# Spectral MLP kernel: the opening put in another order, with bias and weight sums on GpSimd

## Chip, core and metric

The kernel runs on one core of one Trainium2 chip. The metric is the device time of one execution in microseconds; a version's time is the median of its runs.

## What is computed

```python
X = np.fft.rfft(x, axis=1)                      # x: (8, 3008, 256) f32
Yr = Xr @ w_r - Xi @ w_i + b_r                  # 256 x 256 weights
Yi = Xr @ w_i + Xi @ w_r + b_i
Y = soft_threshold(Yr, 0.01) + 1j * soft_threshold(Yi, 0.01)
y = np.fft.irfft(Y, n=3008, axis=1).reshape(24064, 256)
h = y @ w_in                                    # w_in: 256 x 2048, float64
out = np.maximum(0.01 * h, h) @ w_out           # w_out: 2048 x 256, float64
```

## The kernel before

3008 is 47 x 64, so each Fourier transform is a stage over 47 points (A, `fwd`), a stage over 64 (B, in `mid`), the complex weight product and the threshold (`proj`), and the inverse stages G (in `mid`) and the last one (`inverse`, just ahead of the MLP). Between stages the data is turned through DRAM: `fwd(b)` writes `u_dram` and `mid(b)` reads it back as `u`; `mid(b)` writes `v_dram` and `v_load` reads it as `vin`.

`mid(b)` goes over 12 pairs of frequencies. For each, TensorE does stage B into a bank `psh`; ScalarE copies it to `ef` and VectorE adds the third row of `ef`; TensorE multiplies `ef` with three weight matrices (`wr`, `wn` = -(w_r + w_i), `wd` = w_i - w_r) into a bank `pso` (then copied to `kc`) and into both halves of a bank `psf`; VectorE makes `t` = `psf` + `kc`, clamps it to `c` and subtracts `c` from `t`; ScalarE writes the parts of `t`, with signs, to `zf`; TensorE does stage G on `zf` and ScalarE copies the result to `v`, which two DMAs store. There are two banks each of `psf` and `pso`, two buffers of `kc` and three of `u`. In the later batches `t` = `psf` + `kb`, where `kb` = bias + `kc` is made by GpSimd. In batch 0 the bias comes by two more matmuls per pair: a row of ones (`ones`) against a tile `bz`, which holds the bias in two parts.

The MLP uses products of float32 in three passes of high and low parts: `yh`, `yl` against `win_hi`, `win_lo` (line 92), and `gh`, `gl` against `wout_hi`, `wout_lo` (line 576). w_in and w_out come as float64 and are converted here. `load_win(c)` loads a quarter of w_in; `convert_win(c)` splits float64 words (`float64_parts`: two reads by ScalarE, five steps by VectorE), adds the parts into `cva`, makes four sums `ws` of its quadrants for a product of seven terms, and writes high and low parts. `load_wout` does the like for w_out in eight pieces, of which the n-th is needed in the n-th step of the MLP and two steps later. `split_consts` makes high and low parts of the weights and small constants, which the batches after the first use.

The opening, lines 648 to 715, runs batch 0's `fwd`, loads and converts the quarters of w_in, runs batch 0's `mid`, weaves in batch 1's `fwd` (`stage_a1`, called turn here) and then `inverse` and `forms` for the first 512 tokens. The program text gives an order, and a scheduler places instructions on the engines by its own estimates of time; `tc.issue_after` keeps what is inside it behind a named instruction. Each engine, and each DMA queue, then works in its order. A DMA that SyncE or ScalarE starts waits, in that queue, for what it reads and for its buffer.

Tiles share buffers by `tag`: of the tag `e` there is one buffer, and of most others two.

Of the kernel before, what the change touches and what calls it, by code (L numbers as in the profile page):

```python
# [30 lines left out]
def spectral_mlp_kernel(  # L31
# [125 lines left out]
    def convert_win(c):  # L157


        a, q, s = win_tmp  # L160
        float64_parts(win_raw[c], a, q)
        dve.tensor_add(a, a, q)
        a = a.rearrange("p (j q i m) -> p j q i m", j=NH, q=2, i=2)
        a11, a12, a21, a22 = (a[:, j, :, i] for i in range(2) for j in range(2))
        dve.tensor_add(s[:, 0], a21, a22)
        dve.tensor_sub(s[:, 2], a11, a21)
        dve.tensor_sub(s[:, 1], s[:, 0], a11)
        dve.tensor_sub(s[:, 3], a12, s[:, 1])
# [6 lines left out]
    def load_wout():  # L175
# [5 lines left out]
        def load(early):  # L181
# [3 lines left out]
            with tc.issue_after(reads[13 if early else -1].ins):  # L185
                sync.dma_start(raw.rearrange("p (a f) w -> p a (f w)", a=n), ov[:, k * n:(k + 1) * n, :])
# [24 lines left out]
    reads, written, turned, turning, thresholded = [], [], [], [], []  # L211
# [4 lines left out]
    def fwd(b):  # L216
# [5 lines left out]
        def load(c):  # L222
# [89 lines left out]
    def mid(b):  # L312
# [49 lines left out]
        def proj(j):  # L362
# [4 lines left out]

            for dst, c, w in ((0, 2, "wr"), (0, 1, "wn"), (D, 0, "wd")):
# [4 lines left out]
                ] + ([((ones,), (bz[:, D if c == 0 else 0:][:, :D],))] if b == 0 and c < 2 else []))  # L373
# [3 lines left out]
                if c == 2 and b:  # L377
# [16 lines left out]
            for i in range(2):  # L394
# [4 lines left out]
                else:  # L399
                    act.mul(zf[64:, i, :], t[s, 1, :], sign[s, NK1 + j:NK1 + j + 1])  # L400
# [11 lines left out]
        def stage_g(j):  # L412
# [6 lines left out]
            for c in range(2):  # L419
                act.dma_start(vd[c, 2 * j:2 * j + 2, :N2, :].rearrange("k n d -> n k d"), v[c * N2:(c + 1) * N2])  # L420
# [238 lines left out]
    brow = sb.tile([P, 2 * D], F32, name="brow", tag="kb", bufs=1)
    for p in (0, 32):  # L660
        for r, src in enumerate((b_r, b_i)):
            sync.dma_start(brow[p:p + 1, r * D:(r + 1) * D], src.unsqueeze(0))
    sign = const.tile([P, NK1 + NPAIR], F32, name="sign")
    sync.dma_start(sign, sg)
    sync.dma_start(consts["gb32"][0], gb)

    bo = sb.tile([P, 2 * D + P], F32R, name="bz", tag="t", bufs=1)
    bz, ones = bo[:, :2 * D], bo[:, 2 * D:]
    dve.memset(ones.bitcast(F32), 1.0)
# [12 lines left out]
    with tc.issue_after(turned[0].ins):  # L682
        split_consts()
# [159 lines left out]
```

## Time and profile before

| | us |
|---|---|
| median of three runs | 2604.21 (2603.88 to 2604.37) |
| the profiled execution | 2600.34 |
| its span | 2598.6 |
| TensorE busy | 2537.5 (98%) |
| VectorE busy | 1897.1 (73%) |
| ScalarE busy | 1668.5 (64%) |
| GpSimd busy | 229.6 (9%) |

The profile is one execution. Times in it are in microseconds from the start of the span. A timeline has for each instruction its start and its length, and in brackets how long its engine had been idle and what ended that. A table of stages has for each stretch how long every engine was busy. A name as u<-u_dram is a tile with what it is made from, L343 a line of the kernel before; `x24` counts records merged into a row, of which a matmul of float32 has two. Two neighbouring instructions of VectorE overlap by some 0.08 us, so the step from one start to the next is what an instruction costs there.

### The profile page before, as it was taken

The numbers are of one execution on the slowest core, as the hardware profiler recorded it, in microseconds if no ns is written. First come the engines' busy times: TensorE is split into PE (matmuls) and PEld (weight loads), VectorE is DVE, ScalarE is ACT, GpSimd is POOL, SyncE is SP. The second block draws the span as 40 slices with busy tenths as digits, with TensorE's granted clock in tenths as the row PEclk, the third lists the DMA queues.
The fourth block names the chain that finished last, engine by engine and source line by source line (L and its number), as shares of the span: only waits on it lengthen the run. The fifth ranks groups of instructions, "written<-read, shape, count | busy, mean of one in ns | idle before, by whom it ended". The sixth has DMA issues, their size and how long they took to land.

```text
span 2598.6 us, 42643 instructions
## 1 busy us (share of the span) xinstructions
PE 2537.5 (98%) x16300; PEld 2281.5 (88%) x16300; DVE 1897.1 (73%) x3403; ACT 1668.5 (64%) x3174; POOL 229.6 (9%) x180
## 2 busy tenths in 40 slices
PE   5999999999999999999999999999999999999999
PEld 4689888999889998899988999889998889999998
DVE  7687786776777778777786777877777777767675
ACT  5766665776556666567665666566666667655564
POOL 0001121100110001100021000210002000000000
PEclk8999999999999999999999999999999999999999
DMA  8621132111221113211132111321113221101000
GB/s 259 179 85 50 48 89 72 54 47 48 82 78 49 45 41 90 75 55 51 33 97 68 49 49 37 104 67 49 49 36 101 64 58 48 44 17 32 9 17 17
DMA packets 119912, 165.13 MB, mean 64 GB/s; under 512 B 13601, under 2 KB 69917, under 8 KB 119709
## 3 DMA queue, kind: packets, MB, share of 16 engines
q1 hardware_dynamic: 79120, 115.55, 14.6%
q10 hardware_dynamic: 40589, 46.87, 7.1%
q8 instruction: 128, 2.10, 0.4%
q14 instruction: 75, 0.61, 0.1%
HBM read 86.60 MB, written 75.76 MB: 62 GB/s over the span
## 4 chain that ended last, share of the span: by engine, by line
PE 89%; DVE 3%; DMA 2%; ACT 1%; issue 0%; ACTq 0%; SPq 0%; DVEq 0%
PE pso L576 38%; PE psh L92 34%; PE psf L78 11%; PE psf L480 3%; PE psf L343 3%; DMA u<-u_dram 1%; DMA u_dram<-xin 1%; DVE yl L506 0%; DVE gl L563 0%; DMA raw<-w_out_dram 0%; DVE gf L557 0%; ACT gh L561 0%; DVE yt L511 0%; ACT gf L559 0%; DVE yc L512 0%
## 5 line engine op out<-in xcount | busy, mean ns | idle before, releaser
L92 PE MATMUL psh<-yh,win_hi 128*128 128x256 f32 x2632 | 752.3, 286 | 13.8 <-DVE gf L546 10.6
L92 PE MATMUL psh<-yl,win_hi 128*128 128x256 f32 x2632 | 738.3, 280 | 0.6 <-DVE yl L506 0.5
L92 PE MATMUL psh<-yh,win_lo 128*128 128x256 f32 x2632 | 737.9, 280 | 0.0
L576 PE MATMUL pso<-gh,wout_hi 128*128 128x512 f32 x1504 | 593.9, 395 | 0.0
L576 PE MATMUL pso<-gl,wout_hi 128*128 128x512 f32 x1504 | 591.1, 393 | 0.5 <-DVE gl L563 0.5
L576 PE MATMUL pso<-gh,wout_lo 128*128 128x512 f32 x1504 | 590.4, 393 | 0.0
L563 DVE TENSOR_TENSOR gl<-gf,gh 128x1024 fp32r<-128x1024 f32 x376 | 471.8, 1255 | 92.7 <-ACT gh L561 90.6
L92 PEld LDWEIGHTS psh<-yh,win_hi 128*128 128x128 f32 x2632 | 497.0, 189 | 30.7 <-DVE gf L546 15.4
L92 PEld LDWEIGHTS psh<-yl,win_hi 128*128 128x128 f32 x2632 | 497.0, 189 | 12.5 <-DVE yl L506 1.0
L92 PEld LDWEIGHTS psh<-yh,win_lo 128*128 128x128 f32 x2632 | 496.6, 189 | 0.2
L557 DVE TENSOR_TENSOR gf<-psh,u 128x512 f32<-128x512 f32 x376 | 259.1, 689 | 256.3 <-PE psh L92 255.1
L561 ACT CAST gh<-gf 128x1024 fp32r<-128x1024 f32 x376 | 396.4, 1054 | 7.1
L559 ACT ACTIVATE gf<-gf 128x768 f32<-128x768 f32 x376 | 320.0, 851 | 49.5 <-DVE gf L557 47.7
L576 PEld LDWEIGHTS pso<-gl,wout_hi 128*128 128x128 f32 x1504 | 282.5, 188 | 62.9 <-DVE gl L563 1.0
L576 PEld LDWEIGHTS pso<-gh,wout_hi 128*128 128x128 f32 x1504 | 283.1, 188 | 46.9 <-ACT gh L561 0.4
L576 PEld LDWEIGHTS pso<-gh,wout_lo 128*128 128x128 f32 x1504 | 282.9, 188 | 44.9
L556 ACT ACTIVATE gf<-psh 128x256 f32<-128x256 f32 x376 | 145.5, 387 | 266.6 <-PE psh L92 246.9
L542 ACT COPY p<-psh 128x256 f32<-128x256 f32 x376 | 140.1, 373 | 220.2 <-PE psh L92 219.1
L379 POOL TENSOR_TENSOR kb<-bias,kc 128x512 f32<-128x512 f32 x84 | 119.0, 1417 | 1530.6 <-ACT kc L376 1409.6
L543 DVE TENSOR_TENSOR u<-psh,p 128x256 f32<-128x256 f32 x376 | 158.6, 422 | 105.8 <-ACT p L542 103.5
L545 DVE TENSOR_TENSOR gf<-psh,u 128x256 f32<-128x256 f32 x376 | 159.3, 424 | 29.7 <-PE psh L92 2.0
L546 DVE TENSOR_TENSOR gf<-psh,gf 128x256 f32<-128x256 f32 x376 | 159.1, 423 | 9.0
(134 smaller groups left out, 3253.2 us busy)
## 6 DMA issues: line engine op xcount, KB each, us to landing
u<-u_dram SPq DMA_DIRECT2D x192, 128.0 KB, 2.7
v_dram<-v ACTq DMA_DIRECT2D x192, 128.0 KB, 2.4
out_dram<-ob SPq DMA_DIRECT2D x94, 256.0 KB, 2.1
vin<-v_dram SPq DMA_DIRECT2D x96, 240.0 KB, 3.5
xin<-x_dram SPq DMA_DIRECT2D x90, 240.0 KB, 3.0
u_dram<-xin ACTq DMA_DIRECT2D x72, 240.0 KB, 2.4
u_dram<-xin SPq DMA_DIRECT2D x24, 240.0 KB, 3.9
raw<-w_out_dram SPq DMA_DIRECT2D x8, 512.0 KB, 5.0
```

What stands on the lines that cost most here:

```text
L78: last = nc.tensor.matmul(dst, a, b, start=(i == 0), stop=(i == len(terms) - 1))
L92: mlp[:] = [nc.tensor.matmul(dst, a, b, start=start and i == 0, stop=i == 2, skip_group_check=True)]
L542: act.copy(p1, b1[:, lo])
L543: dve.tensor_add(u2, b1[:, hi], p1)
L545: dve.tensor_add(g[:, 3], b2[:, hi], u2)
L546: dve.tensor_add(g[:, 3], b2[:, lo], g[:, 3])
L556: act.activation(g[:, 0], b1[:, lo], AF.Prelu, alpha=SLOPE)
L557: dve.tensor_add(g[:, 1:3], b2.rearrange("p (k n) -> p k n", k=2), u2.unsqueeze(1).broadcast_to([P, 2, HT]))
L559: act.activation(g[:, 1:4], g[:, 1:4], AF.Prelu, alpha=SLOPE)
L561: cp = act.copy(gh, g)
L563: parted[:] = [cp, dve.tensor_sub(gl, g, gh.bitcast(F32))]
L576: mlp[:] = [nc.tensor.matmul(po, a[:, f, s], r[:, i], start=(f == 0 and j == 0), stop=(f == NF - 1 and j == 2),)]
```

## The change

Lines move by a few: what is line 379 before is line 381 after, and 165 to 168 are 167 to 170.

- The quarters 1 to 3 of w_in, the weights, the small constants and all but the first five blocks of `fb` are loaded behind the writes of `u_dram`; the rest of `fb` and quarter 1 behind the first u loads.
- The `ones` row and `bz` go. Batch 0 uses `kb` on GpSimd as the others do.
- In `convert_win` the addition and the four sums go from VectorE to GpSimd.
- Quarter 0 is converted behind the last copy of turn. Quarters 1 and 2 are converted in the middle stage behind the sign products (`signed`), quarter 3 behind the middle stage with a `cva` in the buffer of `e`. `split_consts` moves into the middle stage.
- Batch 0's stores of `v` go from ScalarE's queue to SyncE's.
- One conversion of w_out moves from ahead of the MLP into it, and its first loads are tied to the latest u load.

```diff
@@ convert_win
         a, q, s = win_tmp
+        if c == 3:
+            a = sb.tile([P, NH * NIN], F32, name="cva", tag="e", bufs=1)
         float64_parts(win_raw[c], a, q)
-        dve.tensor_add(a, a, q)
+        pool.tensor_add(a, a, q)
...
-        dve.tensor_add(s[:, 0], a21, a22)
-        dve.tensor_sub(s[:, 2], a11, a21)
-        dve.tensor_sub(s[:, 1], s[:, 0], a11)
-        dve.tensor_sub(s[:, 3], a12, s[:, 1])
+        pool.tensor_add(s[:, 0], a21, a22)
+        pool.tensor_sub(s[:, 2], a11, a21)
+        pool.tensor_sub(s[:, 1], s[:, 0], a11)
+        pool.tensor_sub(s[:, 3], a12, s[:, 1])
@@ load_wout
-            with tc.issue_after(reads[13 if early else -1].ins):
+            with tc.issue_after(reads[-1].ins):
@@ proj
-                ] + ([((ones,), (bz[:, D if c == 0 else 0:][:, :D],))] if b == 0 and c < 2 else []))
+                ])
...
-                if c == 2 and b:
                     kb = sb.tile([P, 2, D], F32, name="kb", tag="kb", bufs=1)
                     pool.tensor_add(kb, bias, kc.unsqueeze(1).broadcast_to([P, 2, D]))
...
-            c = sb.tile([P, 2, D], F32, name="c", tag="kb", bufs=1)
-            if b == 0:
-                dve.tensor_add(t, ps_y.rearrange("p (r d) -> p r d", r=2), kc.unsqueeze(1).broadcast_to([P, 2, D]))
-            else:
-                dve.tensor_add(flat(t), ps_y, flat(kb))
+            c = sb.tile([P, 2, D], F32, name="c", tag="kb" if b else "yt", bufs=1)
+            dve.tensor_add(flat(t), ps_y, flat(kb))
@@ stage_g
-                act.dma_start(vd[c, 2 * j:2 * j + 2, :N2, :].rearrange("k n d -> n k d"), v[c * N2:(c + 1) * N2])
+                (act if b else sync).dma_start(
+                    vd[c, 2 * j:2 * j + 2, :N2, :].rearrange("k n d -> n k d"), v[c * N2:(c + 1) * N2])
@@ the opening
-    load_win(0, (sync, act))
-    load_plain("fb", fb, [P, NK1 + 1, N2])
-    load_weights()
-    brow = ...
+    load_win(0, (sync, sync), xload[0])
+    consts["fb"] = const.tile([P, NK1 + 1, N2], F32, name="fb")
+    sync.dma_start(consts["fb"][:, :5], fb[:, :5])
...
     f0.finish()
-    load_win(1, (sync, sync), written[7])
+    with tc.issue_after(written[-1].ins):
+        load_weights()
+        sync.dma_start(consts["gb32"][0], gb)
...
-    convert_win(0)
     with tc.issue_after(turned[0].ins):
-        split_consts()
+        act.mul(fa32[:, 2], fa32[:, 1], -1.0)
+        convert_win(0)
     m0 = Stream(mid(0), MID)
     m0.to(0.001)
-    for c in range(2, 4):
-        load_win(c, (sync, sync), reads[3])
...
+    with tc.issue_after(reads[3].ins):
+        sync.dma_start(consts["fb"][:, 5:], fb[:, 5:])
+    load_win(1, (sync, sync), reads[3])
...
-    with tc.issue_after(turned[0].ins):
-        convert_win(1)
...
-        if i in (3, 8):
-            convert_win(2 + i // 8)
+        if i in (1, 4):
+            load_win(2 + i // 4, (sync, sync), reads[-1])
+        if i in (3, 7):
+            with tc.issue_after(signed[-1].ins):
+                convert_win(1 + i // 4)
+        if i == 9:
+            with tc.issue_after(thresholded[-1].ins), tc.issue_after(signed[-1].ins):
+                split_consts()
...
     m0.finish()
+    convert_win(3)
...
     next(wout)
-    next(wout)
```

What follows is the order of instructions at three places. First SyncE's DMA queue around the last writes of `u_dram` (`xin` to `u_dram`) and the first loads of `u`; `win_raw` are halves of a quarter of w_in, `w_105` and `w_169` hold the weights and `gb`. Before:

```order
L665 DMA w_105<-gb_dram 128x128
L267 DMA u_dram<-xin 120x512 x7
L155 DMA win_raw<-w_in_dram 128x1024
L267 DMA u_dram<-xin 120x512 x3
L155 DMA win_raw<-w_in_dram 128x1024
L267 DMA u_dram<-xin 120x512
L267 DMA u_dram<-xin 120x256 x2
L329 DMA u<-u_dram 64x2x256 x6
L155 DMA win_raw<-w_in_dram 128x1024 x4
```

After:

```order
L271 DMA u_dram<-xin 120x512 x11
L271 DMA u_dram<-xin 120x256 x2
L121 DMA w_169<-w_r_dram 128x2x256
L121 DMA w_i<-w_i_dram 128x2x256
L664 DMA w_169<-gb_dram 128x128
L333 DMA u<-u_dram 64x2x256 x6
L677 DMA bias<-b_r_dram 128x256
L677 DMA bias<-b_i_dram 128x256
L679 DMA fb<-fb_dram 128x1280
L155 DMA win_raw<-w_in_dram 128x1024 x2
```

The quarter of w_in that lay among the writes now comes behind the u loads, and the weights lie between the writes and the u loads.

Then GpSimd from the start of its work to the middle stage (`kb` is bias + `kc`, `cva` and `ws` belong to `convert_win`). Before:

```order
L317 MEMSET zero 48x256 x2
L379 ISA
L379 TENSOR_TENSOR kb<-bias,kc 128x512 x11
L317 MEMSET zero 48x256
L379 TENSOR_TENSOR kb<-bias,kc 128x512
```

After:

```order
L321 MEMSET zero 48x256
L164 ISA
L164 TENSOR_TENSOR cva<-cva,cvq 128x1024
L167 TENSOR_TENSOR ws<-cva 128x256
L168 TENSOR_TENSOR ws<-cva 128x256
L169 TENSOR_TENSOR ws<-ws,cva 128x256
L170 TENSOR_TENSOR ws<-cva,ws 128x256
L381 TENSOR_TENSOR kb<-bias,kc 128x512 x4
L164 TENSOR_TENSOR cva<-cva,cvq 128x1024
L167 TENSOR_TENSOR ws<-cva 128x256
L168 TENSOR_TENSOR ws<-cva 128x256
L381 TENSOR_TENSOR kb<-bias,kc 128x512
```

Before, its first `kb` is that of batch 1; after, the first row of work is quarter 0's addition, and a `kb` of batch 0 can stand behind the additions of a quarter.

Last VectorE where batch 0's middle stage begins (`ef` is the third row of `ef`, `win_lo` a low part of w_in, `t` and `c` belong to the threshold). Before:

```order
L348 TENSOR_TENSOR ef<-ef 128x2x128
L137 TENSOR_TENSOR cvq<-cvq,win_raw 128x1024
L348 TENSOR_TENSOR ef<-ef 128x2x128
L162 TENSOR_TENSOR cva<-cva,cvq 128x1024
L165 TENSOR_TENSOR ws<-cva 128x256
L166 TENSOR_TENSOR ws<-cva 128x256
L167 TENSOR_TENSOR ws<-ws,cva 128x256
L172 TENSOR_TENSOR win_lo<-cva,win_hi 128x2x256
L172 TENSOR_TENSOR win_lo<-cva,win_hi 128x256
L168 TENSOR_TENSOR ws<-cva,ws 128x256
L348 TENSOR_TENSOR ef<-ef 128x2x128
L172 TENSOR_TENSOR win_lo<-ws,win_hi 128x4x256
```

After:

```order
L122 TENSOR_TENSOR w_169<-w_i,w_169 128x512
L123 SCALAR_TENSOR_TENSOR w_169<-w_i,w_169 128x512
L137 TENSOR_TENSOR cvq<-cvq,win_raw 128x1024
L352 TENSOR_TENSOR ef<-ef 128x2x128 x2
L174 TENSOR_TENSOR win_lo<-cva,win_hi 128x2x256
L174 TENSOR_TENSOR win_lo<-cva,win_hi 128x256
L174 TENSOR_TENSOR win_lo<-ws,win_hi 128x4x256
L389 TENSOR_TENSOR t<-psf,kb 128x512
L390 TENSOR_SCALAR c<-t 128x512
L352 TENSOR_TENSOR ef<-ef 128x2x128
L391 TENSOR_TENSOR t<-t,c 128x512
```

Quarter 1 stood here before; after, it is quarter 0, its sums are gone from VectorE, the weights are made ready in the same place (L122, L123), and the first `t` stands behind the quarter's last piece.

## Rows read from the trace of the kernel before

**Rows 1.** The page, totals of the engines: busy us, share of span, instructions:

```profile
PE 2537.5 (98%) x16300; PEld 2281.5 (88%) x16300; DVE 1897.1 (73%) x3403; ACT 1668.5 (64%) x3174; POOL 229.6 (9%) x180
```

**Rows 2.** Stages: length, then each engine's busy us, granted clock, DMA share, GB/s:

```profile
2.00:36.40 34.40, 13.91 (x28) 5.75 (x28) 22.43 (x36) 16.89 (x30) 0.00 (x0) 0.84 0.92 293
39.90:104.50 64.60, 59.84 (x288) 48.01 (x289) 49.32 (x87) 48.23 (x96) 0.30 (x1) 0.95 0.67 192
60.00:80.00 20.00, 18.91 (x97) 14.98 (x97) 18.09 (x34) 18.33 (x38) 0.00 (x0) 1.00 0.82 247
104.50:128.70 24.20, 24.07 (x84) 13.15 (x82) 13.17 (x29) 14.81 (x32) 0.00 (x0) 0.94 0.75 220
128.70:180.00 51.30, 46.38 (x273) 39.35 (x272) 49.13 (x98) 34.16 (x63) 0.00 (x0) 0.97 0.33 96
```

**Rows 3.** Timeline of TensorE: start, us, operation, [idle before, what ended it]:

```profile
39.91 5.86 PE L343 MATMUL psh<-fb,u 128*128 128x128 f32 x24 [16.76 <-DMA u<-u_dram]
...
87.41 1.03 PE L78 MATMUL psf<-w,ef 128*128 128x256 f32 x4
88.28 1.03 PE L78 MATMUL pso<-w,ef 128*128 128x256 f32 x4
88.95 0.47 PE L78 MATMUL psf<-bz 128*128 128x256 f32 x1
89.26 1.02 PE L78 MATMUL psh<-zf,w 128*128 128x512 f32 x2
...
104.53 8.41 PE L78 MATMUL psh<-xin,fa 120*120 120x512 f32 x16
```

**Rows 4.** Timelines of ScalarE and of SyncE's DMA queue before the middle stage:

```profile
17.65 1.14 ACT L131 ACTIVATE cvq<-win_raw 128x1024 f32<-128x1024 uint32 x1 [2.17 <-DMA win_raw<-w_in_dram]
...
30.30 1.41 SPq L267 DMA_DIRECT2D u_dram<-xin  x3
36.38 3.94 SPq L329 DMA_DIRECT2D u<-u_dram  x6
```

**Rows 5.** Timeline of VectorE in the middle stage:

```profile
76.71 0.69 DVE L388 TENSOR_TENSOR t<-psf,kc 128x512 f32<-128x512 f32 x1
77.31 1.22 DVE L162 TENSOR_TENSOR cva<-cva,cvq 128x1024 f32<-128x1024 f32 x1
78.44 0.43 DVE L391 TENSOR_SCALAR c<-t 128x512 f32<-128x512 f32 x1
78.77 0.42 DVE L165 TENSOR_TENSOR ws<-cva 128x256 f32<-128x256 f32 x1
...
101.10 0.69 DVE L392 TENSOR_TENSOR t<-t,c 128x512 f32<-128x512 f32 x1
```

**Rows 6.** Timelines of VectorE and GpSimd beside each other, later batches:

```profile
333.70 1.29 POOL L379 TENSOR_TENSOR kb<-bias,kc 128x512 f32<-128x512 f32 x1 [15.01 <-ACT kc L376]
333.73 2.34 DVE L563 TENSOR_TENSOR gl<-gf,gh 128x1024 fp32r<-128x1024 f32 x1
...
372.46 2.25 POOL L246 TENSOR_TENSOR xin<-xin,xin 120x512 f32<-120x512 f32 x1
373.64 1.36 DVE L254 CAST xz<-xs 120x512 fp32r<-120x512 f32 x1
...
215.47 1.44 POOL L379 TENSOR_TENSOR kb<-bias,kc 128x512 f32<-128x512 f32 x1 [19.15 <-ACT kc L376]
215.66 0.43 DVE L546 TENSOR_TENSOR gf<-psh,gf 128x256 f32<-128x256 f32 x1
```

**Rows 7.** Groups by line and shape, whole span: count | busy us, mean ns:

```profile
L563 DVE TENSOR_TENSOR gl<-gf,gh 128x1024 fp32r<-128x1024 f32 x376 | 471.8, 1255 | 92.7 <-ACT gh L561 90.6
L254 DVE CAST xz<-xs 120x512 fp32r<-120x512 f32 x36 | 17.3, 481 | 5.6 <-PE psf L78 5.1
L246 POOL TENSOR_TENSOR xin<-xin,xin 120x256 f32<-120x256 f32 x6 | 4.5, 742 | 0.5
```

**Rows 8.** Timeline of ScalarE behind the middle stage:

```profile
116.04 0.67 ACT L131 ACTIVATE cvq<-raw 128x512 f32<-128x512 uint32 x1 [3.33 <-DMA raw<-w_out_dram]
```

More of the change, by code (lines that the diff above doesn't have):

```diff
@@ L209, in spectral_mlp_kernel @@
     v_dram = {}
-    reads, written, turned, turning, thresholded = [], [], [], [], []
+    reads, written, turned, turning, thresholded, signed, xload = [], [], [], [], [], [], []
     NX = -(-NS // 2)
@@ L234, in load @@
                 if b == 0:
-                    (act if h else sync).dma_start(t, x[b, h, :, cols])
+                    ld = (act if h else sync).dma_start(t, x[b, h, :, cols])
+                    if not h:
+                        xload[:] = [ld]
                 else:
@@ L399, in proj @@
                 else:
-                    act.mul(zf[64:, i, :], t[s, 1, :], sign[s, NK1 + j:NK1 + j + 1])
+                    signed[:] = [act.mul(zf[64:, i, :], t[s, 1, :], sign[s, NK1 + j:NK1 + j + 1])]
             if b == 0:
@@ L655, in spectral_mlp_kernel @@
     f0.to(0.01)
-    load_win(0, (sync, act))
-    load_plain("fb", fb, [P, NK1 + 1, N2])
-    load_weights()
[L659 to L662, printed above, removed]
+    load_win(0, (sync, sync), xload[0])
+    consts["fb"] = const.tile([P, NK1 + 1, N2], F32, name="fb")
+    sync.dma_start(consts["fb"][:, :5], fb[:, :5])
     sign = const.tile([P, NK1 + NPAIR], F32, name="sign")
     sync.dma_start(sign, sg)
[L665 to L669, printed above, removed]
-    dve.memset(bz.bitcast(F32), 0.0)
     f0.finish()
-    load_win(1, (sync, sync), written[7])
+    with tc.issue_after(written[-1].ins):
+        load_weights()
+        sync.dma_start(consts["gb32"][0], gb)
     pair("win", [P, 7, NQ, P])
@@ L676, in spectral_mlp_kernel @@
         sb.tile([P, 4, 2, P], F32, name="ws", tag="yh"))
-    act.copy(bz[:1], brow[:1])
-    act.copy(bz[32:33], brow[32:33])
-    dve.tensor_sub(bz[32:33], brow[32:33], bz[32:33].bitcast(F32))
-    act.mul(fa32[:, 2], fa32[:, 1], -1.0)
-    convert_win(0)
     with tc.issue_after(turned[0].ins):
-        split_consts()
+        act.mul(fa32[:, 2], fa32[:, 1], -1.0)
+        convert_win(0)
     m0 = Stream(mid(0), MID)
     m0.to(0.001)
-    for c in range(2, 4):
-        load_win(c, (sync, sync), reads[3])
     bias = const.tile([P, 2, D], F32, name="bias")
     with tc.issue_after(reads[3].ins):
-        load_plain("ga", ga, [PA, 2, P])
         for r, src in enumerate((b_r, b_i)):
             sync.dma_start(bias[:, r, :], src.unsqueeze(0).broadcast_to([P, D]))
+    with tc.issue_after(reads[3].ins):
+        sync.dma_start(consts["fb"][:, 5:], fb[:, 5:])
+    load_win(1, (sync, sync), reads[3])
+    with tc.issue_after(reads[3].ins):
+        load_plain("ga", ga, [PA, 2, P])
     fp = Stream(fwd(1), FWD)
-    with tc.issue_after(turned[0].ins):
-        convert_win(1)
     wout = load_wout()
```

## Prediction, made before the changed kernel was run

> **What bounds the kernel now.** I read the engine totals first: TensorE is busy for 98% of the span [rows 1], so whatever moves the start of the steady MLP moves the end one for one, and what stands off TensorE's path costs nothing. Then the table of stages [rows 2] with TensorE's rows [rows 3]: the idle time lies in the first 180 us. TensorE starts the middle stage at 39.91, after 16.76 us idle on the u loads, and leaves it for batch 1's turn at 104.53 [rows 3]; call this second moment M. From M to 128.7 it is full (24.07 of 24.20). From 128.7 to 180 it lacks some 5 us, with VectorE busy for 49.13 of 51.30: there VectorE is the bound, since w_out is converted beside the first MLP steps. In the middle stage three engines are close to full (TensorE 18.91, VectorE 18.09, ScalarE 18.33 of 20 in 60:80) and GpSimd does nothing [rows 2]. So relief of one engine there pays only up to the next one, and the question is whether GpSimd's time is free. The place to see that is where GpSimd works beside VectorE, in the later batches [rows 6].
>
> **Turn's writes first.** The first u load needs all 14 u_dram writes landed. The DMA engines are saturated until then, share 0.92 at 293 GB/s from 2 to 36.4 [rows 2]; SyncE has issued its last write by 31.7 and can issue the u loads only at 36.38, 3.5 us ahead of TensorE's start [rows 4, 3]. The change takes from in front of the last write 640 KB of fb, 512 KB of weights, 64 KB of gb and 1024 KB of w_in: 2.29 MB, at 293 GB/s 7.8 us. ScalarE no longer reads w_in between two turn copies, as it did at 17.65 after waiting 2.17 [rows 4], so the writes do not starve. U loads at 28.6, TensorE at 32.1. Bounds: the weights (0.59 MB, 2.0 us) now lie between the writes and the u loads; I take them as hidden in the 3.5 us, most of which is latency, and keep 0 to 2.0. The 5.86 us for the first 24 passes [rows 3] I leave as they are.
>
> **Bias off TensorE.** 24 matmuls against the ones row go. A group of four passes steps 0.87 without one (87.41 to 88.28) and 0.98 with one (88.28 to 89.26) [rows 3]: 0.11 each, 2.6 us in all, and only where TensorE is the bound. The brow loads, casts and memsets lie under the wait for DMA and cost nothing either way.
>
> **What goes to GpSimd.** Per pair one kb add of 128x512, and per quarter one add of 128x1024 and four of 128x256. GpSimd takes 1.29 for 512 columns and 0.74 for 256 [rows 6, 7], so 0.55 per 256 more and 2.4 for 1024, an estimate from these. A quarter is 2.4 + 4 x 0.74 = 5.4 us, against 1.13 + 4 x 0.33 = 2.5 on VectorE [rows 5]. Is that time free? A kb runs 1.29 from 333.70; VectorE's gl beside it, both inputs in SBUF, takes 2.34 where its mean is 1.26: it stood until GpSimd was done [rows 6, 7]. The CAST at 373.64, one SBUF input, took 1.36 beside GpSimd's add of 2.25, where its mean is 0.48 [rows 6, 7]. The addition at 215.66 reads PSUM and took its usual 0.43 beside a kb [rows 6]. So GpSimd and VectorE's SBUF-only work take turns, instruction by instruction, and only t (psf + kb) may lie beside GpSimd. I cost the two as one resource.
>
> No row has a tensor_scalar (c, L133, L134, L136) beside GpSimd; the nearest is the CAST, also with one input, and it waited, so I count them. If they did not wait, 12 x 0.33 + 8 x 0.60 = 8.8 us would leave the sum below. The Trainium skill ("SBUF — State Buffer", section Who interferes with whom) lists copy, cast and tensor_scalar as operations that can take the port pair shared with GpSimd, namely in a mode that uses both ports, and has the loser blocked for the whole instruction. By that the 8.8 us stay in the sum; no row here shows it for a tensor_scalar.
>
> **The middle stage.** VectorE, in order, stands at L122 for the weights, which land at 28.6 + 2.0 = 30.6, with quarter 0's L137 behind it: L122 and L123 1.2, L137 1.1, so 32.9. GpSimd's add 2.4 and four sums 3.0, with two ef adds and two win_lo pieces taking turns, 1.6: 39.9. ScalarE's cast of ws 1.0 and VectorE's win_lo of it 1.1 stand ahead of the first t, which so starts near 42. TensorE waits for a t only from pair 2 on. From there the shared resource has, by the steps of rows 5 (an instruction of the same length takes the same step): on VectorE 10 ef and 12 c at 0.33, 7.3; 12 subtractions at 0.60, 7.2; quarters 1 and 2, each 3 x 0.60 + 3 x 1.13 + 0.60 + 0.33 = 6.1, 12.2; the weights' splits, moved in here, 2.4; quarter 3's first three, 2.3; in all 31.4. On GpSimd 11 kb, 14.2, and quarters 1 and 2, 10.8; 25.0. Sum 56.4: without any gap it ends at 98.4. From the last subtraction (101.10 to 101.7) to M went 2.8 [rows 5, 3], so M = 101.2. But kb waits for kc, t for kb, ScalarE's casts for GpSimd, and GpSimd's add for L137 with the next kb queued behind it. VectorE was 90% busy in 60:80 [rows 2], with shorter chains than these; I take that: 56.4 / 0.90 = 62.7, M = 107.5, 3.0 **later** than before though the stage began 7.8 earlier. Bounds: 101.2 with no gap, 111.2 at 85%.
>
> SyncE takes over the 24 v writes. A u load then queues behind a v write that waits for its copy, but u loads run two pairs ahead: 0, and 1 if that cover is gone. ScalarE gets queue time back and is not the bound.
>
> **After M.** Quarter 3 still needs L136 and L137 (1.7), 5.4 on GpSimd and its casts. The third piece of w_out is loaded into the buffer of quarter 3's cva, so its load starts some 2 us later against M; ScalarE read it at 116.04 after 3.33 of waiting, ahead of the inverse's copies in order [rows 8]. Batch 1's turn covers TensorE for about 1 of the 2: +1.0, bounds 0 and 4. And one w_out piece (seven VectorE steps, 3.6) moves from the stretch behind M, where VectorE is 54% busy (13.17 of 24.20), into the one where it is 96% busy [rows 2]: between 0 and 3.6, I take +1.9 as no row tells how much of it a later step absorbs.
>
> **Sum.** 3.0 + 1.0 + 1.9 = 5.9 us on the profiled execution's 2600.3 (its span is 2598.6): 2606.2. The three timed runs have their median 3.9 above it: **2610.1**. A difference within 0.2%, 2599.0 to 2609.4, is about what a measurement of this kernel can't tell from no change.
>
> **Rivals.**
> *Faster: the turns cost little.* GpSimd's adds fall into moments when VectorE waits anyway, and the next bound decides. For TensorE that is 32.1 + 64.6 - 2.6 = 94.1. For ScalarE: 48.2 busy before [rows 2], 2.6 of splits new, from about 34, some 6 idle until the first zf and the tail of 2.8: 93.6. M 10.4 earlier, 2.9 lost after it: 2604.2 - 7.5 = 2596.7. For it: GpSimd stood idle, and kb needs only bias and kc. Against it: rows 6, and VectorE's 49.32 busy in that stage before [rows 2]. It decides once the shared work behind the first t is under some 48 us.
> *No change: turns without gaps.* M = 101.2, 3.3 earlier, 2.9 lost after: 2603.8. For it: where nothing else binds an engine can be nearly full, as VectorE in 128.7:180 [rows 2]. Against it: the chains named.
>
> **How the numbers follow.** Forecast 0.52, 0.10 of it below 2609.4; no change 0.25; faster 0.23. So faster 0.23, same 0.25 + 0.10 = 0.35, slower 0.42. Upper end: M at 111.2 gives 6.7, with 1.0 and 1.9 behind it 2613.8, and the weights' 2.0 put it at 2616. Lower end: half of the faster rival may be left out, so 2596.5.
>
> **What would show it.** The first stage-B matmul near 32: right for the writes; above 35: the DMA queue was not the cause. In the middle stage VectorE's SBUF-only operations stretched beyond their usual times, kb above 1.3 in the mean, TensorE under 85% busy, M at 106 to 109. With M below 98 the turns are cheap and the forecast is wrong. After M, the first w_in product about 1 us later against M, and the last w_out piece one MLP step later.

## The result, and the profile after

The changed kernel takes 2607.09 us in the median of 20 runs (2603.75 to 2611.10), the kernel before 2602.37 in 20 runs beside it (2599.43 to 2607.58). The ratio is 1.0019, interval 1.0012 to 1.0025: 4.7 us slower, about the 0.2% that the prediction named as the limit of what can be told. The profiled executions stand at 2606.07 and 2600.34, 5.7 us apart; the prediction had 5.9 on that scale.

The engine totals of the changed kernel, in the form of [rows 1]:

```profile
PE 2537.9 (97%) x16276; PEld 2278.0 (87%) x16276; DVE 1901.2 (73%) x3380; ACT 1663.8 (64%) x3172; POOL 276.5 (11%) x212
```

GpSimd has 46.9 us more, ScalarE 4.7 less, and TensorE nearly the same (24 matmuls of 16300 fewer, 0.4 us more): what was lost is time in which TensorE waits. The stages, to be held against [rows 2] (length, then busy us of TensorE, its weight loads, VectorE, ScalarE and GpSimd, granted clock, DMA share, GB/s):

```profile
39.90:104.50 64.60, 50.14 (x229) 37.13 (x227) 54.72 (x72) 48.30 (x98) 29.91 (x23) 0.97 0.66 179
128.70:180.00 51.30, 45.01 (x264) 36.77 (x263) 48.38 (x97) 34.18 (x65) 0.00 (x0) 1.00 0.32 98
```

In the middle stage TensorE fell from 59.84 to 50.14, VectorE grew from 49.32 to 54.72 although it ran 72 instructions there in place of 87, and GpSimd went from 0.30 to 29.91. TensorE's timeline, with the rows that answer to [rows 3] and each wait over 1.4 us:

```profile
31.19 3.75 PE L347 MATMUL psh<-fb,u 128*128 128x128 f32 x16 [9.59 <-DMA u<-u_dram]
...
44.95 1.13 PE L347 MATMUL psh<-fb,u 128*128 128x128 f32 x8 [2.78 <-DMA u<-u_dram]
...
67.36 1.97 PE L78 MATMUL psf<-w,ef 128*128 128x256 f32 x8 [1.69 <-DVE t L389]
...
72.03 1.13 PE L78 MATMUL psh<-zf,w 128*128 128x512 f32 x2 [1.84 <-ACT zf L399]
...
91.75 3.65 PE L78 MATMUL psf<-w,ef 128*128 128x256 f32 x8 [2.23 <-DVE t L389]
...
103.22 1.13 PE L78 MATMUL psh<-zf,w 128*128 128x512 f32 x2 [1.80 <-ACT zf L399]
...
105.85 2.05 PE L78 MATMUL psh<-zf,w 128*128 128x512 f32 x2 [1.50 <-DVE zf L397]
107.69 9.32 PE L78 MATMUL psh<-xin,fa 120*120 120x512 f32 x20
```

The stage begins 8.72 us earlier (31.19 against 39.91) and ends 3.16 later (107.69 against 104.53). TensorE waits for t, which VectorE makes, for zf, which hangs on it, and once for u. SyncE issues the u loads at 27.37, where it did at 36.38 [rows 4]:

```profile
27.37 3.95 SPq L333 DMA_DIRECT2D u<-u_dram  x6
```

What makes t and zf late is seen where VectorE and GpSimd stand beside each other. GpSimd's timeline:

```profile
39.18 1.27 POOL L381 TENSOR_TENSOR kb<-bias,kc 128x512 f32<-128x512 f32 x1 [1.98 <-ACT kc L379]
...
71.97 1.45 POOL L381 TENSOR_TENSOR kb<-bias,kc 128x512 f32<-128x512 f32 x1 [2.43 <-ACT zf L399]
74.72 1.58 POOL L381 TENSOR_TENSOR kb<-bias,kc 128x512 f32<-128x512 f32 x1 [1.29 <-DVE t L389]
83.81 3.67 POOL L164 TENSOR_TENSOR cva<-cva,cvq 128x1024 f32<-128x1024 f32 x1 [7.52 <-DVE cvq L137]
...
89.00 1.71 POOL L381 TENSOR_TENSOR kb<-bias,kc 128x512 f32<-128x512 f32 x1
90.68 0.90 POOL L169 TENSOR_TENSOR ws<-ws,cva 128x256 f32<-128x256 f32 x1
...
107.84 2.35 POOL L164 TENSOR_TENSOR cva<-cva,cvq 128x1024 f32<-128x1024 f32 x1 [7.30 <-DVE cvq L137]
```

VectorE's timeline beside the second, the third and the sixth of these rows:

```profile
72.32 1.65 DVE L391 TENSOR_TENSOR t<-t,c 128x512 f32<-128x512 f32 x1
...
75.09 1.49 DVE L390 TENSOR_SCALAR c<-t 128x512 f32<-128x512 f32 x1
...
90.92 0.68 DVE L389 TENSOR_TENSOR t<-psf,kb 128x512 f32<-128x512 f32 x1
```

The subtraction at 72.32 takes 1.65 where its usual length is 0.69 [rows 5], and c at 75.09 takes 1.49 in place of 0.43: they end 0.55 and 0.28 us behind GpSimd's kb, which is through at 73.42 and 76.30. The t at 90.92, which reads PSUM, keeps 0.68 beside GpSimd's addition of 90.68. It goes both ways: the addition of 128x1024 takes 2.35 where it starts with VectorE idle (107.84) and 3.67 at 83.81. The Trainium skill ("SBUF — State Buffer", section Who interferes with whom) counts tensor_scalar among the operations that can contend with GpSimd for a shared port pair; no row of before showed it, the row of c does.

Another delay lies in GpSimd's own order. ScalarE's timeline has a copy to kc that is done at 87.28:

```profile
86.93 0.35 ACT L379 COPY kc<-pso 128x256 f32<-128x256 f32 x1
```

Its kb starts only at 89.00, behind a quarter's addition and two of its sums, and TensorE's wait of 2.23 for t follows; a kb at 65.04 stands so too, ahead of the wait of 1.69.

### The profile page after: what moved, and what is told of

The parts are those of the page before. It is cut to its first block, busy times and chain, and to the rows that moved or that the text cites. A ratio compares the mean times of both kernels' runs of the same rounds, so it can differ in the third digit from the quotient of the medians.

```text
span 2604.3 us, 42637 instructions
## 1 busy us (share of the span) xinstructions
PE 2537.9 (97%) x16276; PEld 2278.0 (87%) x16276; DVE 1901.2 (73%) x3380; ACT 1663.8 (64%) x3172; POOL 276.5 (11%) x212
## 4 chain that ended last, share of the span: by engine, by line
PE 87%; DVE 5%; DMA 3%; ACT 3%; issue 1%; SPq 0%; POOL 0%; ACTq 0%; DVEq 0%
PE pso L576 37%; PE psh L92 33%; PE psf L78 11%; PE psf L480 3%; PE psf L347 3%; DMA u<-u_dram 1%; DMA u_dram<-xin 1%; DVE gl L563 1%; DVE yl L506 1%; DMA raw<-w_out_dram 0%; PE psh L78 0%; ACT gf L559 0%; DVE gf L557 0%; DMA win_raw<-w_in_dram 0%; ACT gh L561 0%
## 5 line engine op out<-in xcount | busy, mean ns | idle before, releaser
L92 PE MATMUL psh<-yh,win_hi 128*128 128x256 f32 x2632 | 751.8, 286 | 16.9 <-DVE gf L546 13.4
L576 PEld LDWEIGHTS pso<-gh,wout_hi 128*128 128x128 f32 x1504 | 283.0, 188 | 46.9 <-issue 0.5
L381 POOL TENSOR_TENSOR kb<-bias,kc 128x512 f32<-128x512 f32 x96 | 137.0, 1427 | 1536.2 <-ACT kc L379 1417.7
```

What stands on the lines that cost most here:

```text
L92: mlp[:] = [nc.tensor.matmul(dst, a, b, start=start and i == 0, stop=i == 2, skip_group_check=True)]
L576: mlp[:] = [nc.tensor.matmul(po, a[:, f, s], r[:, i], start=(f == 0 and j == 0), stop=(f == NF - 1 and j == 2),)]
```

## The marks by which the runs are compared

Four marks of each profiled execution separate the stages: the first stage-B matmul, M (the middle stage left), the first down-projection product, and from there to the end. All are from the timelines, in us; the medians are of 5 to 20 runs. The kernel before had medians of 2601.8 to 2603.2 beside the runs of the table, so medians of different lines compare to about 1 us; a single execution, and with it a mark, can stand some us from its median.

| kernel | first stage B | M | first down-projection | from there to the end | median |
|---|---|---|---|---|---|
| before | 39.91 | 104.53 | 140.09 | 2458.5 | 2602.4 |
| after | 31.19 | 107.69 | 141.66 | 2462.6 | 2607.1 |
| sums_vector | 31.03 | 108.93 | 145.34 | 2467.6 | 2615.2 |
| bias_tensor | 31.46 | 108.06 | 146.57 | 2463.6 | 2608.9 |
| both_back | 31.18 | 102.87 | 139.81 | 2457.2 | 2601.8 |
| unread_once | 31.45 | 108.03 | 144.95 | 2457.8 | 2604.5 |
| unread_twice | 31.17 | 116.82 | 155.34 | 2457.8 | 2614.9 |
| kb_vector | 31.13 | 102.21 | 138.00 | 2474.7 | 2618.1 |
| wout_early | 31.12 | 109.36 | 144.02 | 2456.0 | 2602.7 |
| kb_vector_wout | 30.91 | 105.81 | 142.72 | 2460.5 | 2603.0 |
| both_vact | 30.29 | 101.77 | 139.31 | 2464.0 | 2605.6 |
| both_wout | 31.64 | 102.40 | 141.85 | 2455.9 | 2601.2 |
| u_first | 31.50 | 103.14 | 144.15 | 2456.4 | 2599.7 |
| u_first_q3_last | 31.07 | 103.19 | 143.89 | 2455.4 | 2600.0 |

Against the kernel before, the changed kernel's 5.7 us are +3.2 to M, -1.6 from M to the first down-projection, and +4.1 behind it. There are two causes to find, not one. The -1.6 in the middle is read from the two traces, from M to the first down-projection before and after (columns as in the stages above):

```profile
104.53:140.09 35.56, 32.83 (x135) 20.61 (x134) 24.35 (x51) 22.23 (x46) 0.00 (x0) 0.93 0.61 179
107.69:141.66 33.97, 31.08 (x135) 19.43 (x134) 23.84 (x46) 21.29 (x44) 5.94 (x5) 0.98 0.56 168
```

TensorE is idle for about as long (2.7 and 2.9 us), but for the same 135 matmuls it is busy 1.75 us less, at a granted clock of 0.98 in place of 0.93. That the change brought the higher clock was not tested.

## Experiments: the middle stage

The theory was that of the prediction: GpSimd and VectorE take turns on work that lies in SBUF alone. Rival A was the longer chain from kc through kb to t, or the order the scheduler makes of it; rival B the loads and v's writes on SyncE.

**sums_vector** and **bias_tensor** undo one part each, **both_back** the two together.

```diff
@@ sums_vector: convert_win, the four sums likewise
-        pool.tensor_add(a, a, q)
+        dve.tensor_add(a, a, q)
@@ bias_tensor: proj, with bz, ones and brow as before, and kb only where b
-                ])
+                ] + ([((ones,), (bz[:, D if c == 0 else 0:][:, :D],))] if b == 0 and c < 2 else []))
-            dve.tensor_add(flat(t), ps_y, flat(kb))
+                dve.tensor_add(t, ps_y.rearrange("p (r d) -> p r d", r=2), kc.unsqueeze(1).broadcast_to([P, 2, D]))
```

> The changed kernel with one part undone: the five additions and subtractions behind each converted quarter of w_in are back on VectorE; the bias stays with GpSimd. Marks of the changed kernel: middle stage left (M) at 107.69 us, profiled execution 2606.1 us. Theory (VectorE and GpSimd take turns on work that lies in SBUF alone): three quarters take about 5.4 us of GpSimd each (2.35 for 128x1024, 4 x 0.75), 16 us in all, and come back as some 3 us of VectorE each, 9 us; the sum of turns falls by 7 us, so M at 99 to 101 and the time 6 to 8 us below the changed kernel. Rival A (the longer chain kc, kb, t through GpSimd is what costs, not the turns): the bias still goes that way, M stays at 106 to 108 and the time within 2 us of the changed kernel. Rival B (the v writes and loads on SyncE's queue cost it): M stays as well.

> The changed kernel with another part undone: the bias of batch 0 is added by TensorE matmuls again (24 of 0.11 us), the weight sums stay with GpSimd. Theory (turns): 12 GpSimd additions of 0.73 us alone leave the sum, 8.8 us, and 2.6 us come to TensorE, which has room: M at 99 to 102, the time 5 to 8 us below the changed kernel. Rival A (chain through GpSimd): M falls by as much or more, since the hop is gone, 97 to 101; if the weight sums on VectorE (sums_vector) gain nothing and this one all, it is the chain. Rival B (queue of SyncE): M stays at 106 to 108.

> The changed kernel with both parts undone: bias by TensorE, weight sums by VectorE; what is left of the change is the order of the loads, v's writes on SyncE, the fourth quarter behind the middle stage and the third w_out piece later. Theory: the 8.7 us gained at the first stage-B matmul (39.91 to 31.19) reach M whole, since the middle stage then needs its old 64.6 us: M at 94 to 97, the time 9 to 12 us below the changed kernel and 5 to 8 below the kernel before. Rival A (chain) and the turns agree here. Rival B (loads, v writes and u's transfers on one queue cost the gain): M at 103 or later and the time within 2 us of the changed kernel.

Each part alone leaves M where it was, or later (108.93 and 108.06), and both together bring it to 102.87. The first two expectations fell. The one for bias_tensor priced kb at 0.73, which is what 256 columns take; the row at 39.18 above has 1.27 for its 512. But a right price doesn't save the sum: the prediction's 31.4 with 5.0 for two quarters' sums and 14.2 for kb, which is sums_vector, gives at 90% from a first t at 40.40 M = 99.4, 9.5 us too early. Either part of GpSimd's load, in its order, costs as much as both. both_back's own expectation fell too: 94 to 97 was wanted, and 102.87 came, with a median level with before (ratio 0.9997, interval 0.9988 to 1.0006). That M stayed in the first two is what rival B expected of them, but both_back has the same loads and writes on SyncE and is 5 us earlier.

These three differ from each other in the order that the scheduler makes of them on every engine, so they can't tell the turns from rival A. The next two can.

**unread_once** and **unread_twice** add work on GpSimd that nothing reads, to both_back, whose order on the four other engines stays.

```diff
@@ proj, behind kc; the last line in unread_twice alone
+                    if b == 0:
+                        kd = sb.tile([P, 2, D], F32, name="kd", tag="kd", bufs=1)
+                        pool.tensor_add(kd, bias, kc.unsqueeze(1).broadcast_to([P, 2, D]))
+                        pool.tensor_add(kd, kd, bias)
```

> both_back (M at 102.87 us, 2601.8 us), and beside it GpSimd adds bias and kc into a spare tile in each of the 12 pairs of the middle stage: 12 additions of 128x512, 1.27 us each where they run alone, that no other instruction reads. The order of the instructions on TensorE, VectorE, ScalarE and SyncE is that of both_back, row for row. It holds the work of GpSimd without the chain through it. Theory (VectorE and GpSimd in turns on SBUF): VectorE's steps beside them are stretched, M rises by 3 to 6 us to 106 to 109 and the time by as much. Rival A (the chain kc, kb, t, or the order that the scheduler makes of it): nothing waits for these additions, M within 1 us of 102.87 and the time within 1.5 us of both_back.

> As unread_once with two unread additions in each pair, 24 in all, 30 us alone, more than the 25 us that GpSimd has in the changed kernel; again the order on the other four engines is that of both_back. Theory (turns): the loss grows with the work of GpSimd, M at 108 to 114, 5 to 11 us above both_back, time as much. Rival A (chain or order): M within 1 us of 102.87, time within 1.5 us of both_back.

M rises by 5.16 and by 13.95 (3 to 6 and 5 to 11 were expected), and behind the first down-projection all three need the same 2457 to 2458 us. By the ratios to the kernel before (0.9997, 1.0004 with 0.9995 to 1.0013, and 1.0045 with 1.0032 to 1.0058) it is 1.8 and 12.5 us: both_back's profiled execution is near the fastest of its runs, so 5.16 is rather too much, and the first dozen alone would not settle it. The second does. Rival A is out as the sole cause: nobody reads these additions (one of kc's two buffers comes free behind the first of each pair), no wait of TensorE, VectorE or ScalarE before M ends on GpSimd, and the order is the same. Groups of VectorE in 39.9:104.5 (out<-in, shapes, count, then busy us, mean ns, and idle time before them), first of both_back:

```profile
L395 DVE TENSOR_TENSOR t<-t,c 128x512 f32<-128x512 f32 x12 | 8.2, 687 | 0.2
L391 DVE TENSOR_TENSOR t<-psf,kc 128x512 f32<-128x512 f32 x11 | 7.5, 686 | 8.5 <-ACT kc L379 7.9 <-ACT zf L403 0.6
L394 DVE TENSOR_SCALAR c<-t 128x512 f32<-128x512 f32 x11 | 4.8, 438 | 0.1
```

The same three of unread_once:

```profile
L398 DVE TENSOR_TENSOR t<-t,c 128x512 f32<-128x512 f32 x12 | 9.3, 775 | 0.2
L394 DVE TENSOR_TENSOR t<-psf,kc 128x512 f32<-128x512 f32 x12 | 8.1, 686 | 8.5 <-ACT kc L379 8.0 <-ACT zf L406 0.5
L397 DVE TENSOR_SCALAR c<-t 128x512 f32<-128x512 f32 x12 | 7.6, 633 | 0.2
```

and of unread_twice:

```profile
L399 DVE TENSOR_TENSOR t<-t,c 128x512 f32<-128x512 f32 x10 | 11.3, 1126 | 0.2
L398 DVE TENSOR_SCALAR c<-t 128x512 f32<-128x512 f32 x9 | 6.5, 719 | 0.1
L395 DVE TENSOR_TENSOR t<-psf,kc 128x512 f32<-128x512 f32 x9 | 6.1, 684 | 6.1 <-ACT kc L379 6.1
```

The subtraction goes from 687 to 775 and 1126 ns, c from 438 to 633 and 719, and t, from PSUM, stays at 684 to 686: the turns, and what follows from them, moved M here. Twelve additions of 1.27, 15.2 us, cost 1.8 to 5.2 us, and the second twelve 8.8 to 10.7 more. It is no sum of two engines' times; here the loss goes with how much VectorE's own steps grow. Summed over its steps between the first stage-B matmul and M, each against the usual length of its kind in both_back, they grow by 7.9 us in unread_once and by 18.9 in unread_twice, for 5.2 and 14.0 of M.

In sums_vector and bias_tensor the same count gives 6.6 and 7.4, for 6.1 and 5.2 of M. In the changed kernel it gives 14.1, for 4.8 only. There VectorE is also rid of three quarters' sums (2.5 each [rows 5]) and TensorE of 24 matmuls, and kb stands behind the sums on GpSimd; how these add up to 4.8 no run takes apart, so the chain is not excluded as a part of it.

A part of the loss is TensorE's clock. From the first stage-B matmul to M, columns as above (the granted clock is the third from the right), in before, both_back, unread_once and unread_twice:

```profile
39.91:104.53 64.62, 59.87 (x288) 48.00 (x289) 49.31 (x87) 48.23 (x96) 0.30 (x1) 0.95 0.67 192
31.18:102.87 71.69, 61.55 (x289) 49.69 (x290) 53.86 (x95) 51.73 (x104) 0.30 (x1) 0.93 0.68 192
31.45:108.03 76.58, 64.33 (x288) 50.02 (x289) 62.02 (x96) 52.44 (x104) 18.18 (x13) 0.90 0.64 181
31.17:116.82 85.65, 64.61 (x289) 49.69 (x290) 72.54 (x96) 52.34 (x104) 34.36 (x25) 0.90 0.58 164
```

For the same matmuls TensorE is busy 2.8 us longer in unread_once than in both_back, at 0.90 in place of 0.93, and idle 2.1 us longer; in unread_twice it is 3.1 and 10.9. One such stretch of unread_once:

```profile
80.00:84.00 4.00, 4.00 (x12) 2.86 (x10) 4.00 (x10) 1.58 (x4) 0.05 (x1) 0.50 0.87 303
```

After 2.87 us without work, at 78.78, the granted clock is 0.50, the lower of the two levels, and the matmuls take twice as long for some 5 us. Such a wait is then paid a second time, as at the stage's start before (0.50 in 40:44), behind the 16.76 us of idling [rows 3]. both_back has such stretches too (0.64 in 44:48, 0.67 in 80:84).

**kb_vector** is sums_vector with kb on VectorE as well: the chain is kept, and GpSimd has nothing.

```diff
-                    pool.tensor_add(kb, bias, kc.unsqueeze(1).broadcast_to([P, 2, D]))
+                    (pool if b else dve).tensor_add(kb, bias, kc.unsqueeze(1).broadcast_to([P, 2, D]))
```

> sums_vector (M at 108.93 us, 2615.2 us) with the addition of bias and kc on VectorE too, so that GpSimd has nothing in the middle stage, while the chain kc, kb, t is the same and the additions have no matmuls. Beside VectorE's other work 12 x 0.69 = 8.3 us of it take the place of 12 x 1.27 = 15.2 us of GpSimd (1.6 each as sums_vector's trace has them). Theory (turns): the sum of turns falls by 7 us and no step is stretched: M at 102 to 105, the time 4 to 9 us below sums_vector. Rival A (chain): the same chain, M at 107 to 110.

M came to 102.21, 6.7 below sums_vector, as the turns have it and the chain doesn't: 8.3 us more on VectorE are cheaper than 15.2 on GpSimd. The time did the opposite, 2618.1; what was lost lies behind the first down-projection (2474.7), and belongs to the second cause.

**both_vact** returns v's writes to ScalarE's queue, for rival B.

```diff
-                (act if b else sync).dma_start(
+                act.dma_start(
```

> both_back with the writes of v on ScalarE's queue again, as in the kernel before. In both_back ScalarE waits 4.3 us for these writes (4 times, 1.6 at most), and TensorE 2.87 us for ScalarE's copy of v. Theory: v's writes on SyncE, behind the loads of u and x there, cost part of the gain of the earlier start: M 1 to 3 us below 102.87, the time 1 to 3 us below both_back. Rival (ScalarE's time for issuing 24 writes costs as much as the waits, or the writes wait for the transfers ahead of them on any queue): M within 1 us of 102.87 or later, time within 1.5 us.

M is 1.1 earlier (101.77), at the low end of what was expected, while the time, expected 1 to 3 us shorter, is some 4 us longer, again behind the first down-projection (2464.0), in an order that this edit also changed. V's writes on SyncE are no large part of the loss before M.

## Experiments: behind the middle stage

**wout_early** has the second w_out piece ahead of the expert loop again.

```diff
     for _ in forms(0):
         pass
     next(wout)
+    next(wout)
```

> The changed kernel with the second piece of w_out ahead of the expert loop again, as in the kernel before. Theory (the shift of that piece costs about 3 us in the first MLP steps, where TensorE was busy 6.78 of 10 us in 160 to 170): M unchanged at 107 to 108, the time 2 to 4 us below the changed kernel. Rival (the shift is free, the 3 us come from elsewhere, as from the granted clock): time within 1 us of the changed kernel, or 1 to 2 us above it because the third raw load waits for the buffer that the fourth quarter of w_in now uses.

The median is 4.4 us below the changed kernel's (ratio to before 1.0001, interval 0.9993 to 1.0010), of which the stretch behind the first down-projection gives 6.6 (2456.0 for 2462.6), while M is 1.7 later; both lie just outside what was expected. Two stretches of the early MLP, columns as in the stages above, in the kernel before:

```profile
160.00:170.00 10.00, 9.39 (x62) 8.40 (x62) 10.00 (x21) 7.50 (x14) 0.00 (x0) 1.00 0.18 49
180.00:190.00 10.00, 10.00 (x74) 9.43 (x73) 6.80 (x13) 6.88 (x15) 1.29 (x1) 1.00 0.10 28
```

in the changed kernel:

```profile
160.00:170.00 10.00, 6.78 (x41) 5.71 (x39) 9.94 (x21) 7.21 (x12) 0.00 (x0) 1.00 0.09 29
180.00:190.00 10.00, 7.75 (x48) 6.73 (x47) 9.89 (x20) 6.09 (x11) 0.00 (x0) 1.00 0.11 28
```

and in wout_early:

```profile
160.00:170.00 10.00, 7.79 (x53) 7.04 (x53) 9.98 (x22) 7.36 (x15) 0.00 (x0) 1.00 0.30 101
180.00:190.00 10.00, 10.00 (x64) 9.00 (x64) 8.54 (x18) 5.38 (x10) 1.29 (x1) 1.00 0.09 26
```

In the changed kernel VectorE is full in both stretches and TensorE idles for 3.2 and 2.3 us. Its waits in the first:

```profile
162.95 0.38 PE L92 MATMUL psh<-yh,win_hi 128*128 128x256 f32 x1 [1.64 <-DVE gf L546]
...
170.04 0.39 PE L92 MATMUL psh<-yh,win_hi 128*128 128x256 f32 x1 [1.62 <-DVE gf L546]
```

The `gf` it waits for is a step of the MLP on VectorE, and conversions of w_out stand between these steps, one conversion more behind the first down-projection than before. With the piece back, 180:190 is full again; 160:170 is not (7.79), and there one wait, of 2.21 at 166.33, is for a u load.

**kb_vector_wout** asks whether kb_vector's loss is of this kind.

```diff
@@ kb_vector, in the opening
     next(wout)
+    next(wout)
```

> kb_vector with the second w_out piece ahead of the expert loop. kb_vector left the middle stage at 102.21 us, as the turns have it, and yet took 2618.1 us: from its first down-projection product (138.00) to its end are 2474.7 us, where wout_early and both_wout have 2456.0 and 2455.9. Theory (that loss comes from where the w_out conversions stand among VectorE's steps of the first MLP steps, and the piece's place sets it): M at 102 to 105, 2455 to 2459 us behind the first down-projection product, the time 2596 to 2601 us. Rival (kb on VectorE costs it some other way, all through the kernel): 2468 us or more behind that product, the time 2608 us or more.

It is: 14.2 of the 16.2 us that it lacked against the kernel before are gone (2460.5 for 2474.7), and the time falls from 2618.1 to 2602.95. Both marks and the time miss the theory's bounds by a little (105.81 for 102 to 105, 2460.5 for 2455 to 2459, 2602.95 for 2596 to 2601), on the theory's side. M itself moved by 3.6 us between two kernels that do the same work ahead of it, so an order alone is worth that much there, and about half of the 6.7 us between sums_vector and kb_vector may be that.

But the piece's place is not the whole rule. both_back, with the late piece, needs 2457.2, and kb_vector, with the same late piece, 2474.7. The variants with the early piece lie at 2455.4 to 2456.4, but for kb_vector_wout; with the late one it depends on how the scheduler lays the conversions between the MLP's steps, and that changed with every edit. Which step of kb_vector's order costs it most was not tried.

## Experiments: where the earlier start went

both_back has the load order without GpSimd's work, starts at 31.18 and reaches M only 1.7 us before the kernel before. TensorE's rows at its waits:

```profile
44.84 1.82 PE L347 MATMUL psh<-fb,u 128*128 128x128 f32 x8 [3.20 <-DMA u<-u_dram]
...
78.01 1.12 PE L78 MATMUL psh<-zf,w 128*128 128x512 f32 x2 [2.87 <-ACT v L421]
...
101.93 1.10 PE L78 MATMUL psh<-zf,w 128*128 128x512 f32 x2 [3.21 <-DVE zf L401]
102.87 8.73 PE L78 MATMUL psh<-xin,fa 120*120 120x512 f32 x16
```

The waits behind the start are 3.2 for u, 2.87 for v, 0.86 for zf and 3.21 for the last zf, 10.1 us, where before had 4.6. That is 5.4 of the 7.1 us that were lost on the way to M; the other 1.7 are TensorE's longer busy time (61.55 against 59.87 in the stages above), at the lower clock. What ScalarE did ahead of the v at 77.38 that TensorE waits for:

```profile
74.97 0.62 ACT L112 CAST wr_hi<-w 128x512 fp32r<-128x512 f32 x1
...
76.73 0.48 ACT L112 CAST fa_hi<-fa 120x120 fp32r<-120x120 f32 x2
77.11 0.36 ACT L379 COPY kc<-pso 128x256 f32<-128x256 f32 x1
77.38 0.58 ACT L421 COPY v<-psh 128x512 f32<-128x512 f32 x1
```

Six casts of `split_consts`, which the change moves into the middle stage, 2.1 us, stand ahead of kc and v in its order. That they cause the wait was not tested by moving them.

Three kernels tried to get more out of the start: **both_wout** (both_back with the `next(wout)` that wout_early adds), **u_first** (quarter 1 of w_in behind the fourth pair of u on SyncE) and **u_first_q3_last** (quarter 3's VectorE steps behind the last threshold).

```diff
@@ u_first, on top of both_wout
-    load_win(1, (sync, sync), reads[3])
...
     for i in range(1, 17):
         m0.to(i / 16)
+        if i == 1:
+            load_win(1, (sync, sync), reads[-1])
@@ u_first_q3_last, on top of u_first
-    convert_win(3)
+    with tc.issue_after(thresholded[-1].ins):
+        convert_win(3)
```

> both_back with the second w_out piece ahead of the expert loop, as in wout_early. both_back leaves the middle stage (M) at 102.87 us, and from its first down-projection product at 139.81 to its end are 2457.2 us; wout_early has 2456.0 there, the changed kernel 2462.6. Theory: GpSimd's part is gone from the middle stage and w_out's part from the MLP, so M at 102 to 105 and the rest at 2455 to 2458: the time within 2 us of both_back's 2601.8, 1 us below it if anything. Rival: both parts add up fully (5.3 and 4.4 us below the changed kernel): 2597 to 2598.

> both_wout with the second quarter of w_in issued behind the fourth pair of u on SyncE instead of ahead of it; the order on the other engines is the same. In both_back TensorE waits 3.20 us for u at 44.84 and then runs some 4 us at half its clock. Theory (the early start of the stage is not used, since u stands behind 1 MB of w_in and 0.64 MB of fb in the queue): that wait falls to under 1 us, M comes 2 to 4 us earlier than both_wout's, and the time by 2 to 4 us. Rival (all 16 DMA engines are busy from 42 to 70 us in any order, so the wait only moves to w_in's second quarter or to later pairs of u): M within 1 us of both_wout's, time within 1 us.

> u_first, and VectorE's steps for the fourth quarter of w_in put behind the threshold of the last pair; in both_back two of them (L133, L134) stand among the last pair's four steps, and TensorE waits 3.21 us for zf just ahead of M. Theory: that wait falls by 1.3 to 2 us and M by as much against u_first; the first w_in product follows M and not the fourth quarter, so the time falls by 0 to 2 us. Rival (the fourth quarter is then late for the first w_in product, or the MLP's order shifts with it): M earlier by as much, the time the same or 1 to 3 us longer.

both_wout did as expected: M 102.40, 2455.9 behind the first down-projection, 2601.2. The parts don't add up fully; with GpSimd's work gone, the late piece had cost both_back little. TensorE's rows in u_first:

```profile
41.08 1.16 PE L347 MATMUL psh<-fb,u 128*128 128x128 f32 x8 [1.11 <-DMA fb<-fb_dram]
...
50.54 1.13 PE L347 MATMUL psh<-fb,u 128*128 128x128 f32 x8 [0.46 <-DMA u<-u_dram]
...
63.47 1.13 PE L78 MATMUL psh<-zf,w 128*128 128x512 f32 x2 [1.85 <-DMA v_dram<-v]
...
73.33 1.12 PE L78 MATMUL psh<-zf,w 128*128 128x512 f32 x2 [0.44 <-DMA u<-u_dram]
```

The wait of 2.80 for u that both_wout has at 44.70 became four: 1.11 for fb, 0.46 and 0.44 for u and 1.85 for a v write, 3.9 us, and M came no earlier (103.14, 0.7 later). For M the rival held: what is put ahead of one transfer is missing from the next. The time is 1.5 us lower, between the rival's 1 and the theory's 2 to 4. Nor did the last zf's wait fall by more than 0.6 (3.22 to 2.63) in u_first_q3_last, whose M is 103.19; that theory fell. By their ratios to before, 0.9991 (0.9982 to 1.0000) and 0.9990 (0.9982 to 0.9999), these two are the fastest here, some 7 us below the changed kernel and about 2.5 below the one before, just at the edge of what can be told. Nor is the early start lost ahead of M alone: from M to the first down-projection both_back needs 36.9 us, both_wout 39.5 and u_first 41.0, where before had 35.6. So both_wout and u_first come to that product later than before, and what they gain lies behind it. Which step costs it was not tried.

## Why the prediction was right, point by point

- **First stage-B matmul**: 32.1 foretold, 31.19 found, and with it the reason, 2.29 MB less ahead of the last u_dram write (u loads at 27.37, 28.6 foretold). The first t stood at 42 in the text and starts at 41.46.
- **M**: 107.5 foretold, 107.69 found. The mechanism was right in kind: SBUF-only steps were stretched (subtractions 1173 ns in the mean, c 599), kb took 1447 ns in the mean, TensorE was busy for 50.14 of 64.60, 78%. The open question of the tensor_scalar is answered by c's 1.49: it waits. But the sum that gave 107.5 is not a law. Applied to sums_vector it gives M 9.5 us too early, and in both_back, where nothing is shared, TensorE's own bound (31.2 + 64.6 = 95.8) is 7 us too early, by 5.4 us of waits and 1.7 of slower matmuls. So the hit on M was luck. Two errors cancelled: against the rival in which the turns cost little (M = 94.1, 10.4 earlier) the earlier start was worth 1.7 us, and GpSimd's work, on top of that, cost 4.8 us and not the 13.4 that lie between 94.1 and 107.5. The steps that failed are "u loads run two pairs ahead: 0" (TensorE waited 2.78 for a u load with fb and w_in ahead of it in the queue), ScalarE as "not the bound" (in both_back TensorE waited 2.87 for its copy of v, with six casts ahead of it), the clock, at which TensorE's 64.6 us were taken over unchanged, and the fill of 90% that stood for all of this.
- **After M**: +1.0 foretold for the third w_out piece. ScalarE did read it later against M (121.05, M + 13.4, where it was M + 11.5 [rows 8]), yet the first down-projection came at M + 33.97 and not at M + 35.56: -1.6 in place of +1.0, and the first w_in product at M + 18.62 where it was M + 19.43, not 1 us later. The 1.6 go with TensorE's clock, 0.98 for 0.93, and not with the piece. In both_back, which reads the piece later too (M + 15.0), the stretch is 1.4 longer, near the term's +1.0.
- **The piece moved into the MLP**: +1.9 foretold within 0 to 3.6, +4.1 found behind the first down-projection, and wout_early gets 6.6 back there. The term was mis-sized: it took VectorE's 3.6 us as a bound, while the runs have more than that for one piece, in an order that moved with it.
- **The sum**: 3.0 + 1.0 + 1.9 against 3.16 - 1.6 + 4.1. The total is right to 0.2 us on the profiled execution; of its three terms one is right and two are off by 2 to 3 us in opposite directions, which is luck as well. The time foretold was 2610.1; of the 3.0 us to the measured 2607.1, 1.8 lie in the kernel before, whose median is 2602.37 beside these runs and was 2604.21.
- **Rivals**: "the turns cost little" is excluded for this stage by unread_twice; kb_vector against sums_vector points the same way. What the change does without GpSimd's part is both_back: no difference from before.

## What to carry to other kernels

Before work is moved to an idle engine, look for rows in which that engine and the relieved one run beside each other; where the steps of one stretch until the other is through, the move can lengthen the relieved engine's other steps by more than it takes away, as here by 14.1 us for some 7.5 us of sums, and its price is not read from the idle engine's free time. An earlier start is worth only what the rest of the stage can follow: list the stage's other waits first, since they may grow when the first one goes, as here from 4.6 to 10.1 us. And where a scheduler orders the program, an edit's price is read best from one that leaves the order alone, such as an operation that nobody reads, and every other edit by marks, stage by stage, because the order elsewhere moves with it.

## What the runs showed of the hardware that was not expected

- The turns stretch GpSimd too: its 128x1024 addition took 2.35 where it started with VectorE idle and 3.67 in company, and kb 1.27 and up to 1.71, so work on GpSimd can't be priced by its length alone either.
- Behind the wait of 2.87 us in unread_once the granted clock stood at 0.50 for the next 4 us, and behind 3.20 us in both_back a group of eight matmuls took 1.82 us in place of 1.05. Behind 2.78 us in the changed kernel (44.95) it took 1.13.
- The price of the turns is not proportional: 1.8 to 5.2 us for the first 15.2 us of GpSimd's work, 8.8 to 10.7 for the second.
